# The gates of four chunks, two chunks at a time, by seven block products in place of eight

## Chip, core and metric

The kernel runs on one core of one Trainium2 chip. The metric is the device time of one execution in microseconds, the median of several runs. The core's engines work in parallel, each through its own instruction queue and in order: TensorE (PE, with its weight loads shown as PEld), VectorE (DVE), ScalarE (ACT), GpSimd (POOL) and SyncE (SP), which here issues nearly all DMAs. Matrix products land in PSUM, which has eight banks of 128 x 512 float32; DVE and ACT read them from there.

## The reference

Linear attention over 8 batches of 8 heads, 576 positions and 64 dimensions, then a feed-forward layer whose hidden value is the largest of three products. Cut to what matters:

```python
q_s = softmax(q, axis=-1)          # over the 64 dimensions
k_s = softmax(k, axis=2)           # over the 576 positions
kv = np.einsum('bhsd,bhse->bhde', k_s, v)
attn = np.einsum('bhsd,bhde->bhse', q_s, kv)
x = attn.transpose(0, 2, 1, 3).reshape(4608, 512)
h = np.maximum(np.maximum(x @ w1, x @ w2), x @ w3)     # each w: 512 x 768
out = h @ w_out                                        # 768 x 512
```

The weights come as float64 and the result goes out as float32.

## The kernel before

**Precision.** A product of two float32 matrices is made of three matmuls in a rounded format (F32R): each operand is split into a high part, which ACT copies, and a low part, which DVE subtracts; low x high, high x low and high x high are added up in one PSUM bank.

**Chunks.** The 4608 rows of x are worked on in nine chunks of 512. Chunks 0 to 7 are the first 512 positions of the eight batches; chunk 8 holds the 64 left over of each batch (the tile `left`). x lies turned: the 512 inner values in four blocks of 128 partitions (`g`, one for each pair of heads), the 512 rows along the free dimension.

**Gates** (`Chunk.gate`, L821 to 838). For each of six blocks of 128 hidden features (`j`) and each of three weights (`i`), 4 inner blocks x 3 = 12 matmuls of 128x128 on 128x512 add up in one of four banks (pool `pf`): 216 matmuls a chunk. **Hidden** (`Chunk.hidden`, L840): ACT copies the first product out of its bank, DVE takes the maximum with the other two, ACT makes the high part, DVE the low part. **Second products** (`Chunk.second`, L863): for each of four tiles of 128 rows 6 x 3 = 18 matmuls, a copy by ACT (L892) and a store by SP (L899, L904), the last tile in two halves (L880, L883): 72 matmuls a chunk.

**Attention.** Each batch has four pairs of heads. For batches 2 to 7 a pair takes loads of k, q and v (14 DMAs with the transfers of `q`), DVE and ACT work for the two softmaxes, a 32x32 transpose by DVE into `tb` (L654), eight small SP transfers `qT<-tb` (L667) that finish the turning of q, a split of q (L676, L679), the k v product on PE (L532) and the product that gives x (`Pair.x_steps`, L714 to 762), six matmuls at L741. From its bank x is split into `xbuf[b % 2]`, so batch b's x waits for the gates of chunk b - 2 (L721), and 64 rows go to `left`. Batches 0 and 1 go another way, by PE transposes. `left_queries` (L764) makes the left-over rows of these two.

**Weights.** 24 slices of w1, w2, w3 and w_out are loaded as float64, joined to float32 and split into `wh`, `wl` and `wo` in the first 110 us or so; `wh` and `wl` then stay in SBUF.

**Order.** The whole order is made when the program is built. Every piece of work is a generator that yields steps (`Step`: engine, estimated cost, what it waits for, which buffers it takes and frees). The planner (`Streams.run`, L149) holds a clock for each engine and always issues the next step that can begin, the one of lowest rank where several can. Ranks are set at the end (L992 to 1038): chunk c's gates have 1000 + 100 c and its second products 50 more, hidden steps come first of all, attention has the low ranks in the order of batches. Each engine then runs its instructions in just this order on the chip, and waits where a semaphore isn't there yet. The banks of `pf` are passed on in one fixed sequence, `in_pf` (L311).

Of the kernel before, what the change touches and what calls it, by code (L numbers as in the profile page):

```python
# [49 lines left out]
X_F32 = False  # L50

# [153 lines left out]
def linear_attention_then_maxout_ffn(  # L205
# [43 lines left out]

    const = ctx.enter_context(tc.tile_pool(name="const", bufs=1))  # L250
    att = ctx.enter_context(tc.tile_pool(name="att", bufs=2))
    hp = ctx.enter_context(tc.tile_pool(name="hp", bufs=NJ))
# [4 lines left out]
    start_stack, early_stack, conv2_stack = ExitStack(), ExitStack(), ExitStack()  # L257
    start = start_stack.enter_context(tc.tile_pool(name="start", bufs=2, side="right"))

    wh = [const.tile([P, NC, DF], F32R, name=f"wh{i}") for i in range(3)]  # L260
    wl = [const.tile([P, NC, DF], F32R, name=f"wl{i}") for i in range(3)]
    wo = []
    left = const.tile([P, 2, NC, B * LEFT], F32R, name="left")
    xbuf = [const.tile([P, 2, NC, CH], F32R, name="x0")]
# [6 lines left out]
    early = early_stack.enter_context(tc.tile_pool(name="early", bufs=1))  # L271
    k0 = early.tile([P, 5, H, D], F32, name="k0")
    q0 = early.tile([P, H, 4, D], F32, name="q0")
    v0 = early.tile([P, H, 5, D], F32, name="v0")
# [8 lines left out]
    count = early.tile([P, P], F32, name="count")  # L283
    turned_count = early.tile([P, P], F32, name="turned_count")
# [27 lines left out]
    for c in range(B + 1):  # L312
        in_pf += [(c, j, i) for j in range(NJ) for i in range(3)] + [(c, "y", t) for t in range(4)]
    st = Streams({"pf": 4, "pa": BANKS[0], "sm": BANKS[1], "keT": 1, "hp": NJ, "tmp": 3, "ke": 2, "kep": 1, "qe": 2, "qf": 1, "qt": 2, "tb": 1, "qT": 2, "qhl": 1}, {"pf": in_pf, "tb": list(range(TURNED * NP, B * NP))})
    late_pools, turn_pools = [], []
# [3 lines left out]
    class Slice:  # L319
# [18 lines left out]
        def load(self, pool, nst, nx):  # L338
            t = pool.tile([P, NC, 2 * P], U32, name="wst", bufs=nst)
# [3 lines left out]
            self.pool, self.nx = pool, nx  # L343

        def join(self, room):
            n, low, high = self.n, self.low, self.high
            e = yield Step("AV", (0.56, 0.39), [("wst", n)], take=[(room, n)], port="V")
            x = self.x = self.pool.tile([P, CH], F32, name="wx", bufs=self.nx)
# [32 lines left out]


    class Pair:
# [330 lines left out]
        def x_steps(self):  # L714
# [6 lines left out]
            after = [("bd", n), ("qhl", n), ("gates", b - 2) if b >= 2 else None, "late" if b == 1 else None]  # L721
# [20 lines left out]
            h, lo = (xbuf[b % 2][:, i, self.g, :] for i in range(2))  # L742
# [6 lines left out]
            rest = CH - half  # L749
            yield Step("A", act(half))  # L750
            nc.scalar.copy(out=h[:, :half], in_=xT[:, :half])
            yield Step("A", act(rest))
            nc.scalar.copy(out=h[:, half:], in_=xT2[:, :rest])
            yield Step("V", dve(half), free=[room])
            nc.vector.tensor_sub(out=lo[:, :half], in0=xT[:, :half], in1=h[:, :half].bitcast(F32))
            yield Step("V", dve(rest), gives=("x", b, self.g))
            nc.vector.tensor_sub(out=lo[:, half:], in0=xT2[:, :rest], in1=h[:, half:].bitcast(F32))
            h, lo = (left[:, i, self.g, b * LEFT : (b + 1) * LEFT] for i in range(2))
            yield Step("A", act(LEFT))
            nc.scalar.copy(out=h, in_=xT2[:, rest:half])  # L760
            yield Step("V", dve(LEFT), free=[small], gives=("xl", b, self.g))
            nc.vector.tensor_sub(out=lo, in0=xT2[:, rest:half], in1=h.bitcast(F32))

    def left_queries():  # L764
# [41 lines left out]
        h, lo = (left[:, i, :, 0 : TURNED * LEFT] for i in range(2))  # L806
        yield Step("A", act(CH))
        nc.scalar.copy(out=h, in_=xv)
        yield Step("V", dve(CH), free=room, gives="left")
        nc.vector.tensor_sub(out=lo, in0=xv, in1=h.bitcast(F32))  # L810


# [258 lines left out]
```

## Time and profile before

| | |
|---|---|
| median of three runs | 703.74 us (703.21 to 704.28) |
| the profiled execution | 704.3 us, span 702.2 us |
| matmul instructions | 3542 |
| DMA bytes moved | 58.06 MB, 83280 packets |
| HBM read, written | 40.89 MB, 9.44 MB |
| gate matmuls, mean duration | 392 ns (wh), 398 ns (wl) |

The span is the time from the first to the last instruction; 2.1 us of the execution lie around it. A matmul's duration is longer than the spacing of two, since matmuls overlap. In the page, the slices cut the span in forty parts, each digit a share in tenths. In the chain that ended last each row is a start, a length, the engine and the line, with the number of instructions merged. In a group's row the columns after the bar are the total busy time, the mean of one in ns, and the idle time before them with its releaser. In the windows each engine's busy time stands with its instruction count, then PE's granted clock, the share of the DMA engines and GB/s.

### The profile page before, as it was taken

Reading aid. Unit: us, or ns where it says so; the run is one execution under the profiler, and the core shown is the slowest. Engines: PE = TensorE matmul, PEld = TensorE weight load, DVE = VectorE, ACT = ScalarE, POOL = GpSimd, SP = SyncE. Lnnn points to the kernel's source line nnn. Section 1 sums busy time; section 2 is a strip of 40 time slices with the busy share of each in tenths; the row PEclk is TensorE's granted clock in tenths of the full one; section 3 lists DMA queues with packets and bytes.
Section 4 is the critical chain, followed back from the end, with each engine's and each line's share of the span. In section 5 each row is a group of like instructions: output and inputs, shape, how many; then the busy total and the mean of one; then the engine's idle time right before and its main releaser. Section 6 shows DMA issues by size and latency. Waiting matters only on the chain.

```text
span 702.2 us, 9785 instructions
## 1 busy us (share of the span) xinstructions
PE 675.4 (96%) x3542; PEld 551.7 (79%) x3542; DVE 398.5 (57%) x804; ACT 249.1 (35%) x578; POOL 58.5 (8%) x75
## 2 busy tenths in 40 slices
PE   3589999999999999999999999999999999999997
PEld 2467877888888888888888888888888888888885
DVE  6689988789869797795588258623222112201220
ACT  5579866334344334331442135113211111111111
POOL 3223222301100000010000000000000000000000
PEclk9789999999999999999999999999999999999999
DMA  8748433443462443440253024101100000010002
GB/s 238 201 147 243 148 95 106 145 107 97 130 167 69 113 116 102 127 112 15 74 153 105 1 70 126 34 1 33 45 1 1 30 31 0 1 46 15 1 0 61
DMA packets 83280, 58.06 MB, mean 83 GB/s; under 512 B 49184, under 2 KB 74784, under 8 KB 83232
## 3 DMA queue, kind: packets, MB, share of 16 engines
q1 hardware_dynamic: 83152, 57.31, 28.9%
q8 instruction: 28, 0.46, 0.3%
q14 instruction: 20, 0.16, 0.1%
q10 hardware_dynamic: 80, 0.13, 0.0%
HBM read 40.89 MB, written 9.44 MB: 72 GB/s over the span
## 4 chain that ended last, share of the span: by engine, by line
PE 93%; DMA 2%; SPq 1%; DVE 1%; ACT 1%; issue 0%; ACTq 0%; DVEq 0%
PE pf L835 64%; PE pf L874 21%; DMA wst<-in_moe_w_dram 2%; PE pa L532 2%; PE pa L741 2%; PE sm L741 1%; PE sm L575 0%; SPq L930 0%; PE pa L464 0%; PE pa L703 0%; PE pa L689 0%; SPq L418 0%; PE pa L804 0%; SPq L933 0%; DVE wl L379 0%
## 5 line engine op out<-in xcount | busy, mean ns | idle before, releaser
L835 PE MATMUL pf<-x,wh 128*128 128x512 f32 x1152 | 358.5, 392 | 0.0
L835 PEld LDWEIGHTS pf<-x,wh 128*128 128x128 f32 x1152 | 216.8, 188 | 47.6 <-issue 0.2
L835 PE MATMUL pf<-x,wl 128*128 128x512 f32 x576 | 229.1, 398 | 0.7 <-ACT bdf L587 0.7
L847 DVE TENSOR_TENSOR m<-pf,m 128x512 f32<-128x512 f32 x108 | 74.4, 689 | 188.0 <-PE pf L835 185.8
L835 PEld LDWEIGHTS pf<-x,wl 128*128 128x128 f32 x576 | 108.4, 188 | 24.9 <-ACT bdf L587 0.9
L850 ACT CAST h_h<-m 128x512 fp32r<-128x512 f32 x54 | 33.5, 620 | 182.4 <-DVE m L847 182.4
L874 PE MATMUL pf<-ol,h_h 128*128 128x512 f32 x216 | 86.2, 399 | 0.0
L874 PE MATMUL pf<-oh,h_l 128*128 128x512 f32 x216 | 84.4, 391 | 0.0
L874 PE MATMUL pf<-oh,h_h 128*128 128x512 f32 x216 | 84.4, 391 | 0.0
L844 ACT COPY m<-pf 128x512 f32<-128x512 f32 x54 | 31.6, 586 | 57.0 <-PE pf L835 52.5
L854 DVE TENSOR_TENSOR h_l<-m,h_h 128x512 fp32r<-128x512 f32 x54 | 37.1, 687 | 19.2 <-ACT h_h L850 19.2
L874 PEld LDWEIGHTS pf<-ol,h_h 128*128 128x128 f32 x216 | 40.6, 188 | 8.8 <-issue 0.7
L874 PEld LDWEIGHTS pf<-oh,h_l 128*128 128x128 f32 x216 | 40.5, 188 | 8.6
L874 PEld LDWEIGHTS pf<-oh,h_h 128*128 128x128 f32 x216 | 40.7, 188 | 8.4 <-issue 0.7
L835 PE MATMUL pf<-left,wh 128*128 128x512 f32 x144 | 44.3, 389 | 0.0
L502 POOL PARTITION_ALL_REDUCE kma<-km x24 | 19.0, 793 | 281.3 <-DVE km L499 131.0
L892 ACT COPY m<-pf 128x512 f32<-128x512 f32 x35 | 20.5, 587 | 56.8 <-PE pf L874 56.3
L364 POOL TENSOR_TENSOR wst<-wx,wst 128x512 int32<-128x512 int32 x24 | 31.3, 1305 | 87.7 <-DVE wx L360 52.8
L654 DVE STREAM_TRANSPOSE tb<-qt 128x576 f32<-128x576 f32 x24 | 30.7, 1281 | 5.4 <-DMA qT<-tb 5.2
L835 PEld LDWEIGHTS pf<-left,wh 128*128 128x128 f32 x144 | 27.0, 188 | 5.6
L835 PE MATMUL pf<-left,wl 128*128 128x512 f32 x72 | 28.0, 389 | 0.0
L679 DVE TENSOR_TENSOR q_l<-qT,q_h 128x576 fp32r<-128x576 f32 x24 | 18.1, 754 | 16.6 <-ACT q_h L676 15.9
(154 smaller groups left out, 671.7 us busy)
## 6 DMA issues: line engine op xcount, KB each, us to landing
wst<-in_moe_w_dram SPq DMA_DIRECT2D x18, 512.0 KB, 4.8
out_dram<-m SPq DMA_DIRECT2D x32, 256.0 KB, 2.2
vt<-in_v_dram SPq DMA_DIRECT2D x56, 128.0 KB, 3.0
qt<-in_q_dram SPq DMA_DIRECT2D x24, 288.0 KB, 3.2
qT<-tb SPq DMA_DIRECT2D x192, 36.0 KB, 1.9
kt<-in_k_dram SPq DMA_DIRECT2D x24, 256.0 KB, 3.1
wst<-in_moe_w_out_dram SPq DMA_DIRECT2D x6, 512.0 KB, 3.3
q<-in_q_dram SPq DMA_DIRECT2D x8, 256.0 KB, 5.5
```

The lines of the kernel that those rows point to most:

```text
L364: nc.gpsimd.tensor_add(out=low.bitcast(I32), in0=x.bitcast(I32), in1=low.bitcast(I32))
L502: nc.gpsimd.partition_all_reduce(kma, km, P, bass_isa.ReduceOp.max)
L654: nc.vector.transpose(out=tb.rearrange("p e (c s) -> p s e c", s=QS), in_=self.qt.rearrange("p s (e c) -> p s e c", e=2))
L679: nc.vector.tensor_sub(out=q_l, in0=self.qT, in1=q_h.bitcast(F32))
L741: nc.tensor.matmul(out=out, lhsT=l, rhs=r[:, cs], start=(i == 0), stop=(i == last))
L835: nc.tensor.matmul(out=ps, lhsT=l[:, cc, js], rhs=r, start=(cc == 0 and t == 0), stop=(cc == NC - 1 and t == 2))
L844: nc.scalar.copy(out=m, in_=self.m.pop((j, 0)))
L847: nc.vector.tensor_max(out=m, in0=self.m.pop((j, i)), in1=m)
L850: nc.scalar.copy(out=h, in_=m)
L854: unit[e].tensor_sub(out=lo, in0=m, in1=h.bitcast(F32))
L874: nc.tensor.matmul(out=po, lhsT=l, rhs=r[:, j, :], start=(j == 0 and i == 0), stop=(j == NJ - 1 and i == 2))
L892: nc.scalar.copy(out=o, in_=po)
```

## The change

Chunks 0 to 4 stay as they were. Chunks 5 and 6, and 7 and 8, are worked on as two pairs (`Duo`). A pair's gates are seen as 2 x 2 blocks: two feature blocks of 128 (j = 2jp and 2jp + 1) by two halves of the inner dimension for a weight, two halves of the inner dimension by two chunks for x. With weight blocks A, x blocks B, and S, T for their sums,

```
S1 = A21 + A22   S2 = S1 - A11   S3 = A11 - A21   S4 = A12 - S2
T1 = B12 - B11   T2 = B22 - T1   T3 = B22 - B12   T4 = B21 - T2
P1 = A11 B11  P2 = A12 B21  P3 = S4 B22  P4 = A22 T4  P5 = S1 T1  P6 = S2 T2  P7 = S3 T3
U = P1 + P6   C11 = P1 + P2   C12 = U + P5 + P3   C22 = U + P5 + P7   C21 = U + P7 + P4
```

Each product is six matmuls (2 inner blocks x 3 terms), where the four outputs took 48. There are nine block pairs `u` (three jp, three weights), so 63 products for each pair of chunks.

- *Weight blocks.* For each u the three plain blocks, high and low, are stored from `wh`, `wl` to DRAM (`prepare_weights`, six DMAs of 128 KB), and the four sums are formed by DVE (six operations and two for the low parts) and ACT (two) and stored (`mix_weights`, two DMAs). Each product then loads its block of 256 KB into one of ten buffers `ws`.
- *x.* Batches 5, 6 and 7 keep x unsplit (`xf`, ACT copies only), as does `left`. `Duo.convert` forms the four sums on DVE and splits seven blocks into `xb`, which lies where the weights were. x of batches 5 and 6 waits for the gates of chunk 3, of batch 7 for the first pair's conversion (`x_free`).
- *Banks.* Four banks: `a` holds P1 and then P1 + P2; `c` holds P5 and then P5 + P3; two others in turn are seeded by ACT with P1 and take P6, P7 and P4. Between products ACT and DVE read or copy them and take the maxima into `mm`.
- *Second products* run after all nine u of a pair, eight tiles, each split first into one of two buffers `hs`.
- *Places.* Most tiles move into one slab with offsets by hand, so that the new ones can share space with weights, x and hidden tiles that are done with.
- `left_queries` gets rank 230, where it had 301.

```diff
+PAIRED = 5
+LEFT_AT, PREP_AT, PREP_STEP = 230.0, 280.0, 0.5
...
+    W_AT, X0_AT, SCR_AT, H_AT, E_AT = 0, 73728, 90112, 98304, 122880
+    xbuf = [place(f"x{i}", [P, 2, NC, CH], F32R, at) for i, at in enumerate((X0_AT, E_AT))]
+    hp_h = Placed("h_h", [P, CH], F32R, H_AT, NJ)
+    wo = [place(nm, [P, NJ, DM], F32R, E_AT + 16384 + 12288 * i) for i, nm in enumerate(("oh", "ol"))]
+    xf = [place(f"xf{i}", [P, NC, CH], F32, E_AT + 8192 * i) for i in range(2)]
+    xb = [place(f"xb{i}", [P, 2, 2, CH], F32R, W_AT + 8192 * i) for i in range(7)]
+    ws = [place(f"ws{i}", [P, 2, 2, P], F32R, SCR_AT + 2048 * i if i < 4 else W_AT + 57344 + 2048 * (i - 4)) for i in (0, 1, *range(4, 12))]
+    mm = place("mm", [P, 2, NJ, CH], F32, H_AT)
+    hs = [place(f"hs{i}", [P, 2, NJ, P], F32R, X0_AT + 6144 * i) for i in range(2)]
+    wd = [dram.tile([P, 7, 2, 2, P], F32, name=f"wd{u}") for u in range(9)]
...
+    for u in range(10):
+        turn = [("P1", u), ("P5", u), ("P4", u - 1), ("P6", u), ("P2", u), ("P3", u), ("P7", u)]
+        wino_order += [(p, n) for p, n in turn if 0 <= n < 9]
...
+    def x_free(b):
+        if b < 2:
+            return None
+        if b < PAIRED:
+            return ("gates", b - 2)
+        return ("gates", PAIRED - 2) if b < PAIRED + 2 else ("conv", b - 2 - (b - PAIRED) % 2)
...
-            after = [("bd", n), ("qhl", n), ("gates", b - 2) if b >= 2 else None, "late" if b == 1 else None]
+            after = [("bd", n), ("qhl", n), x_free(b), "late" if b == 1 else None]
...
+            else:
+                yield Step("A", act(half), free=[room])
+                nc.scalar.copy(out=x[:, :half], in_=xT[:, :half])
+                yield Step("A", act(rest), gives=("x", b, self.g))
+                nc.scalar.copy(out=x[:, half:], in_=xT2[:, :rest])
...
+    WINO = {"P1": (0, 0), "P5": (6, 1), "P2": (1, 2), "P6": (3, 3), "P7": (5, 4), "P3": (4, 5), "P4": (2, 6)}
...
+    def mix_weights():
...
+            for r in range(2):
+                yield Step("V", dve(CH), ["turn", "left", ("split", 6 * jp + i), ("split", 6 * jp + 3 + i)], port="V")
+                nc.vector.tensor_tensor(out=v[:, r], in0=hv[:, r].bitcast(F32), in1=lv[:, r].bitcast(F32), op=ALU.add)
+            for o, x, y, op in (
+                (a22, a21, a22, ALU.add), (a21, a11, a21, ALU.subtract), (a11, a22, a11, ALU.subtract),
+                (a12, a12, a11, ALU.subtract),
+            ):
+                yield Step("V", dve(256), port="V")
+                nc.vector.tensor_tensor(out=o, in0=x, in1=y, op=op)
...
+            for hl, t in enumerate((mix_h, mix_l)):
+                yield Step("S", 0.64, kb=512, gives=("mixed", u) if hl else None)
...
+    class Duo:
...
+        def convert(self):
+            c = self.c
+            before = [("gates", PAIRED - 1), *(("kept", u) for u in range(9))] if c == PAIRED else [("gates", c - 2)]
...
+            def split(i, src, after, gives):
+                yield Step("A", act(2 * CH), [*before, *after])
+                nc.scalar.copy(out=xb[i][:, 0], in_=src)
+                yield Step("V", dve(2 * CH), gives=("cv", c, i), port="V")
+                nc.vector.tensor_tensor(out=xb[i][:, 1], in0=src, in1=xb[i][:, 0].bitcast(F32), op=ALU.subtract)
...
+        def weights(self, at):
+            c = self.c
+            for n, (p, u) in enumerate(self.order):
+                slot = (at + n) % len(ws)
+                first = c == PAIRED and n < len(ws)
+                after = [("mixed", u), ("kept", u), (("mixed", 8) if slot < 2 else ("gates", PAIRED - 1)) if first else None]
+                yield Step("S", 0.64, after, take=[("ws", (c, p, u))], gives=("w", c, p, u), kb=256)
+                nc.sync.dma_start(out=ws[slot].bitcast(F32), in_=wd[u][:, WINO[p][0]])
...
+        def products(self, at):
...
+                need = {
+                    "P1": ("c11", u - 1), "P5": ("c12", u - 1), "P2": ("sb", u), "P6": ("sb", u), "P7": ("u2", u),
+                    "P3": ("s5", u), "P4": ("c22", u),
+                }[p]
...
+                yield Step("T", 6 * f32r(CH), after, take=take, free=[("ws", (c, p, u))], gives=(p, c, u))
...
+                terms = [(k, a, b) for k in range(2) for a, b in ((1, 0), (0, 1), (0, 0))]
+                for i, (k, a, b) in enumerate(terms):
                     nc.tensor.matmul(
+                        out=bank[on], lhsT=w[:, a, k], rhs=x[:, b, k], start=(i == 0 and p in ("P1", "P5")), stop=(i == 5),
+                        skip_group_check=True,
                     )
...
+            return [
+                seeded(),
+                copied("c", s5[u % 2], [("P5", c, u), ago("d22")], ("s5", c, u)),
+                also(alone("a", m11, [("P2", c, u), *(old or ())], ("c11", c, u), bank_free(0, u == 8)), ("d11", c, u)),
+                copied(sb, u2[u % 2], [("P6", c, u), ago("d12")], ("u2", c, u)),
+                with_copy("c", u2[u % 2], m12, [("P3", c, u), ("u2", c, u)], ("c12", c, u), bank_free(1, u == 8), ("d12", c, u)),
+                with_copy(sb, s5[u % 2], m22, [("P7", c, u), ("s5", c, u)], ("c22", c, u), done=("d22", c, u)),
+                alone(sb, m21, [("P4", c, u)], ("c21", c, u), bank_free(2 + u % 2, u >= 7)),
+                met(),
+            ]
...
-    st.add(left_queries(), FIRST + CHUNK * 4)
+    st.add(left_queries(), LEFT_AT)
+    st.add(prepare_weights(), LEFT_AT)
+    st.add(mix_weights(), PREP_AT, PREP_STEP)
...
+    for n, d in enumerate(duos):
+        r = GATES_AT + 100.0 * (PAIRED + 2 * n)
+        for i, g in enumerate(d.convert()):
+            st.add(g, -900.0 + i)
...
+        st.add(d.weights(len(d.order) * n), r - 2000.0)
+        st.add(d.products(len(d.order) * n), r)
+        for u in range(9):
+            for g in d.outcome(u):
+                st.add(g, -1500.0 + u)
...
+        for t in range(8):
+            st.add(d.hidden(t), -1000.0 + t)
+            st.add(d.second(t), r + 50 + t)
```

More of the change, by code (lines that the diff above doesn't have):

```diff
@@ L805, in left_queries @@
         xv = xT.rearrange("p (g t) -> p g t", g=NP)
[L806 to L810, printed above, removed]
+        yield Step("A", act(CH), free=room, gives="left")
+        nc.scalar.copy(out=left[:, :, 0 : TURNED * LEFT], in_=xv)
     class Chunk:
@@ L863, in second @@
         def second(self, t):
-            c, ts = self.c, slice(t * P, (t + 1) * P)
-            for j in range(NJ):
-                key = ("pf", (c, "y", t))
-                yield Step(
-                    "T", 3 * f32r(CH), [("h", c, j), ("split", NG + j)], take=[key] if j == 0 else (), gives=("y", c, t, j)
-                )
-                if j == 0:
-                    po = pf.tile([P, CH], F32, name="pf")
-                hh, hl = self.hh[j][:, ts], self.hl[j][:, ts]
-                for i, (l, r) in enumerate(((hh, wo[1]), (hh, wo[0]), (hl, wo[0]))):
+            ts = slice(t * P, (t + 1) * P)
@@ new lines, in linear_attention_then_maxout_ffn, with prepare_weights @@
+    WINO = {"P1": (0, 0), "P5": (6, 1), "P2": (1, 2), "P6": (3, 3), "P7": (5, 4), "P3": (4, 5), "P4": (2, 6)}
+    def prepare_weights():
+        for u in range(9):
+            jp, i = divmod(u, 3)
+            js = slice(2 * jp * P, 2 * (jp + 1) * P)
+            hv, lv = (t[i][:, :, js].rearrange("p c (r n) -> p r c n", r=2) for t in (wh, wl))
+            yield Step("S", 0.64, ["turn", ("split", 6 * jp + i), ("split", 6 * jp + 3 + i)], kb=128)
+            for part, (block, r, cc) in enumerate(((0, 0, 0), (1, 0, 2), (2, 1, 2))):
+                for hl, t in enumerate((hv, lv)):
+                    if part or hl:
+                        yield Step("S", 0.64, kb=128, gives=("kept", u) if part == 2 and hl else None)
+                    nc.sync.dma_start(out=wd[u][:, block, hl], in_=t[:, r, cc : cc + 2].bitcast(F32))
@@ new lines, in all_gates, with hidden @@
+        def all_gates(self):
+            yield Step("-", 0.0, [("P4", self.c, 8), ("P3", self.c, 8)], gives=("gates", self.c))
+        def hidden(self, t):
+            c = self.c
+            h, q = self.tiles[t]
+            ts = slice(q * P, (q + 1) * P)
+            o = hs[t % 2]
+            for part, jj in enumerate((slice(0, 4), slice(4, NJ))):
+                n = (jj.stop - jj.start) * P
+                yield Step("A", act(n), [("m", c, 5), ("m", c, 8) if part else None], take=[("hs", (c, t))] if not part else ())
+                nc.scalar.copy(out=o[:, 0, jj], in_=mm[:, h, jj, ts])
+                yield Step("V", dve(n), gives=("hl", c, t, part), port="V")
+                nc.vector.tensor_tensor(
+                    out=o[:, 1, jj], in0=mm[:, h, jj, ts], in1=o[:, 0, jj].bitcast(F32), op=ALU.subtract
+                )
@@ L908, in linear_attention_then_maxout_ffn, with second @@
+        def second(self, t):
+            h, q = self.tiles[t]
+            o = hs[t % 2]
+            yield from second_product(
+                self.c, t, lambda j: (o[:, 0, j], o[:, 1, j]), lambda j: [("hl", self.c, t, 0 if j < 4 else 1)],
+                self.c + h, q, last=self.c + 2 > B and t == 7, done=("hs", (self.c, t)),
+            )
     pairs = {(b, g): Pair(b, g) for b in range(B) for g in range(NP)}
     slices = [Slice(n) for n in range(NS)]
-    chunks = [Chunk(c) for c in range(B + 1)]
+    chunks = [Chunk(c) for c in range(PAIRED)]
@@ L911, in linear_attention_then_maxout_ffn @@
+    duos = [Duo(c) for c in range(PAIRED, B + 1, 2)]
     N_ST, N_X, N_ST2, N_X2 = ROOMS
```

297 lines of the change are left out of this document (219 added, 78 removed).

## The prediction

> **What bounds the kernel now.** I read the totals and the forty slices first, then the chain that ended last in order of time, then the groups of instructions by shape.
>
> ```profile
> span 702.2 us, 9785 instructions
> PE 675.4 (96%) x3542; PEld 551.7 (79%) x3542; DVE 398.5 (57%) x804; ACT 249.1 (35%) x578; POOL 58.5 (8%) x75
> PEclk9789999999999999999999999999999999999999
> DMA  8748433443462443440253024101100000010002
> GB/s 238 201 147 243 148 95 106 145 107 97 130 167 69 113 116 102 127 112 15 74 153 105 1 70 126 34 1 33 45 1 1 30 31 0 1 46 15 1 0 61
> PE 93%; DMA 2%; SPq 1%; DVE 1%; ACT 1%; issue 0%; ACTq 0%; DVEq 0%
> ```
>
> PE is busy 96% of the span and carries 93% of the chain. From the third slice on nothing else decides. So the change is worth what it takes out of PE's stream, less every gap that it opens there. The chain from chunk 4's second products to the end:
>
> ```profile
> 406.45 1.36 PE pf L874 x6
> 429.00 50.38 PE pf L835 x216
> 500.60 49.01 PE pf L835 x216
> 549.61 16.33 PE pf L874 x72
> 565.94 50.20 PE pf L835 x216
> 616.14 16.33 PE pf L874 x72
> 632.47 48.97 PE pf L835 x216
> 681.44 16.34 PE pf L874 x72
> 697.85 0.44 DVE m L880
> ```
>
> There are no gaps: 216 gate matmuls a chunk, 72 second ones, the next chunk. 48.97/216 = 0.2267 us a matmul, and 16.33/72 = 0.2268. Chunks 5 and 7 take 0.2333 and 0.2324: they read x from the other of the two buffers. I can't say from this trace what in that buffer costs 2.5%, so it is carried as a pace of its own.
>
> **The change part by part.**
>
> *Removed.* The gates of chunks 5 to 8: 50.38 + 49.01 + 50.20 + 48.97 = 198.6 us, 864 matmuls.
>
> *Added on PE.* Seven products of six matmuls for each of nine block pairs, twice: 2 x 9 x 42 = 756 matmuls of the same shape. At 0.2267 they take 171.4 us, at 0.2333 176.4 us. Net -27.2 us at the better pace. The second products stay at 72 per chunk, and attention's matmuls stay too.
>
> *Pace.* x, the weight blocks, the hidden tiles and the output weights all get new places, so any stage may run at either pace. If chunks 1 and 3 lose the slow pace, that is 2 x (50.2 - 49.0) = -2.4 us. If the products and all nine chunks' second products (648 x 0.0066 = 4.3 us) get it, that is 5.0 + 4.3 = +9.3 us. I take **+2**, near the pace that most of the rows have.
>
> *Handovers inside a product turn.* Each bank is drained or seeded between two products that use it: P1 is copied by ACT into the third bank before P6 adds to it, P6 is read before P7, P7 before P4, P2 before the next P1, P3 before the next P5. Each time two other products, twelve matmuls, lie between: 2.72 us (P5 to P3 has three). PE works in the written order, so whatever stands behind a product that waits, waits too. What the reading takes:
>
> ```profile
> 672.65 0.61 PE L835 MATMUL pf<-left,wh 128*128 128x512 f32 x2
> 673.11 0.39 PE L835 MATMUL pf<-left,wl 128*128 128x512 f32 x1
> 673.31 0.69 DVE L847 TENSOR_TENSOR m<-pf,m 128x512 f32<-128x512 f32 x1 [1.96 <-PE pf L835]
> 674.03 0.62 ACT L850 CAST h_h<-m 128x512 fp32r<-128x512 f32 x1 [5.52 <-DVE m L847]
> L844 ACT COPY m<-pf 128x512 f32<-128x512 f32 x54 | 31.6, 586 | 57.0 <-PE pf L835 52.5 <-issue 4.1
> L654 DVE STREAM_TRANSPOSE tb<-qt 128x576 f32<-128x576 f32 x24 | 30.7, 1281 | 5.4 <-DMA qT<-tb 5.2
> ```
>
> DVE starts 0.20 us after the next group's first matmul (673.31 against 673.11), works 0.69, and the next engine starts 0.03 later. So a handover needs about 0.9 to 1.0 us out of 2.72. It has 1.7 us to spare, more than one 1.28 us transpose of batch 7 in front of it. DVE's load in a turn is six operations of 0.69 (two where i = 0): 3 x 1.4 + 6 x 4.1 = 29 us of 86. Price: 0 if they fit; if a transpose and another operation stand in front at one handover in each turn, 0.3 us x 18 = 5. I take **+1**.
>
> *Weight blocks from DRAM.* 63 loads of 256 KB for each pair, one per product (1.36 us): 193 GB/s.
>
> ```profile
> 600.00:650.00 50.00, 50.00 (x221) 41.11 (x220) 8.44 (x13) 7.63 (x13) 0.00 (x0) 1.00 0.06 22
> 406.40:429.00 22.60, 22.60 (x178) 18.94 (x176) 13.89 (x31) 11.13 (x28) 0.70 (x1) 1.00 0.39 106
> out_dram<-m SPq DMA_DIRECT2D x32, 256.0 KB, 2.2
> wst<-in_moe_w_out_dram SPq DMA_DIRECT2D x6, 512.0 KB, 3.3
> ```
>
> In the windows (last two columns: DMA share, GB/s) 2 KB rows go at 22/0.06 = 370 GB/s of a full DMA, and in the fourth slice 243 GB/s were really moved at a share of 0.8. So the loads take some 0.55 of the DMA, and with attention's densest stage (0.39) still under 1. Ten buffers let a load run 13.6 us ahead, against 2.2 to 3.3 us to land. Price 0, covered by that lead; bounds 0 and +5, should the two overlap for a whole pair.
>
> *Before the first pair: the crowd.* The block sums need eight DVE operations in each of nine rounds, 9 x (4 x 0.69 + 4 x 0.41) = 40 us of DVE, and 18 ACT copies. SP gets 54 + 18 DMAs to issue, at 0.63 each 34 + 11 us. Batch 6's x, which waited for chunk 4's gates, is now needed as those end, to be converted together with batch 5's.
>
> ```profile
> L497 DVE TENSOR_TENSOR kh<-kt 128x256 f32<-128x256 f32 x24 | 9.8, 409 | 2.2 <-DMA kt<-in_k_dram 2.2
> 200.00:250.00 50.00, 50.00 (x298) 41.60 (x298) 39.17 (x83) 18.80 (x41) 2.11 (x3) 1.00 0.41 107
> 250.00:300.00 50.00, 50.00 (x302) 41.51 (x301) 40.00 (x85) 20.76 (x44) 3.11 (x4) 1.00 0.45 121
> 300.00:334.70 34.70, 34.70 (x155) 28.14 (x155) 24.99 (x46) 8.83 (x14) 1.77 (x2) 1.00 0.20 53
> 334.70:357.20 22.50, 22.50 (x178) 18.86 (x176) 13.84 (x31) 11.07 (x27) 0.70 (x1) 1.00 0.37 106
> 357.20:406.40 49.20, 49.20 (x219) 40.74 (x218) 31.03 (x60) 11.86 (x21) 2.40 (x3) 1.00 0.26 70
> 227.76 5.01 SPq L667 DMA_DIRECT2D qT<-tb  x8
> 313.88 26.51 SPq L667 DMA_DIRECT2D qT<-tb  x11
> L741 PE MATMUL pa<-q_l,bdh x8: 292/296/300, 152.0 to 238.6; 128*128 128x288 f32 x8
> 362.48 5.24 SPq L667 DMA_DIRECT2D qT<-tb  x7
> 375.28 36.81 SPq L667 DMA_DIRECT2D qT<-tb  x11
> ```
>
> DVE (third busy figure) is idle 10.8 + 10.0 + 9.7 + 8.7 + 18.2 = 57 us between 200 and 406.4, so 40 us fit on paper, and some 0.8 us a pair goes away with the low parts of x for batches 5 and 6. Is the last pair in time? Pairs of heads follow each other by 12.8 us (375.28 - 362.48). The last of batch 6 began its qT transfers at 375.28, right behind the third, and was then held inside the 36.81 us row until chunk 4's gates had freed room. Not held, it starts near 388, and its x comes 10.8 us after (227.76 to 238.6): 399. Gates of chunk 4 end at 406.45, some 4 us later when batch 6's own matmuls have moved ahead of them, and the second products cover another 16.3. In those the convert needs DVE for ten operations of 1024 elements, which I estimate at 1.25 us each (0.41 for 256, 0.69 for 512), 12.5 us, and the first two products wait for three of them. So about 20 us of slack stand against 85 us of added work on two engines, most of which falls into their idle time. The transfers that were held within rows of 26.51 and 36.81 us show that SP had room, too. Price 0 if the idle time is used well; +15 if 35 of the 85 us find no idle time and come after the slack of 20. I take **+3**, near the end that the idle rows speak for.
>
> *At the end of each pair.* The hidden tiles need all nine rounds. P4 of the last round waits for P7's reading, 1.0 us, and the last two blocks of the first second products then need a max, a copy and a subtraction, 0.9 + 0.4 + 0.4 us. Ready beside it are the first four blocks of two tiles, 2 x 12 x 0.2268 = 5.4 us: covered. The third tile waits for one of two buffers, about 1.7 us after the first tile ends, with 1.4 us of the second left: 0.3 to 1 us. From both sides 0 to 3 for each pair; I take **+2** for both. In the last pair the same tail follows as before (from 697.85 on).
>
> *Sum.* 704.3 in the profiled execution (span 702.2 and 2.1 around it) - 27.2 + 2 + 1 + 0 + 3 + 2 = 685.1. The median of the three runs, 703.74, lies 0.56 below the profiled one: **684.5 us**.
>
> **The rivals.**
>
> *The better case.* The new places run at the fast pace and the covers hold: 703.7 - 27.2 - 2.4 to + 1: 674 to 677. For it speaks how gapless the chain is; against it, that three kinds of waits are new and each has only some 2 us to spare.
>
> *Gaps remain.* Late x for the first pair by 10 to 15 us, or a handover missed in every turn: 688 to 700.
>
> *The clock.* PE that waits a little at every handover could lose clock. What slower means here:
>
> ```profile
> L464 PE MATMUL pa<-ident,k 128*128 128x128 f32 x16 | 4.3, 422 | 5.8 <-DMA k<-in_k_dram 5.8
> L464 PE MATMUL pa<-ident,kt 128*128 128x128 f32 x16 | 2.4, 272 | 0.0
> ```
>
> The same transposes took 422 ns in the first slices, where PEclk shows 7 to 9, and 272 later: 1.55 times. A quarter of the products at that rate costs 0.25 x 0.55 x 171.4 = 24 us: 708. Against it: the gates pass four banks on all the time and PEclk stays at 9, because the next bank is always free. The Trainium skill, "TensorE: Matmul & The Clock Gate", A second HAM failure mode: psum-queue depth-cycling, speaks for this rival: it tells of a kernel that cycled through its banks, where PE idled between groups often enough for the clock to fall and rise again. So far the trace doesn't agree, as the gates cycle through banks without loss.
>
> *The loads bound.* A load that comes every 2.2 us, the time of one 256 KB transfer, gives 126 x 2.2 = 277 us of loads against 171 of products: 790. It turns the sign from 1.58 us a load on (1.36 + 27.2/126). The fourth slice, where 512 KB loads overlap at 243 GB/s (1.08 us for 256 KB), speaks against it. The Trainium skill, "DMA: Bandwidth & Descriptors", Rules for kernel authors, asks for 1 MiB per DMA for full bandwidth; these have a quarter of that.
>
> *Slower by the crowd.* One mechanism before the first pair can turn the sign: SP issues in order, a store of block sums waits there for DVE, and batch 6's q transfers wait behind it; PE's products wait for batch 6's x. Every microsecond by which the last x comes more than the 20 us of slack after 399 is a microsecond of idle PE. It decides from 27 us beyond the slack on, when nearly all of the 85 us find no idle time: 704 to 715. Against it stand 57 us of idle DVE and the two held transfers.
>
> *It doesn't do what it says.* If the planner put the products later than the code's ranks say, nothing would be saved and 703.7 stays; so would it if the gaps eat just what is saved.
>
> **How the numbers follow.** The forecast, 678 to 688: 0.50. The better case, 674 to 678: 0.17. Gaps, 688 to 700: 0.19. The clock: 0.04. The loads: 0.01. The crowd: 0.06. No change: 0.03. The range 675 to 698 leaves out the last four, 0.14, and the edges of the second and third. A measurement of this kernel can tell about 0.2%, 1.4 us. Faster by more than that: 0.50 + 0.17 + 0.19 = 0.86; within it 0.03; slower 0.04 + 0.01 + 0.06 = 0.11.
>
> **What would show it.** Two stretches of 378 product matmuls of about 86 us each in the chain, with 145 us of second products, attention and tail around them after chunk 4's gates; PE's waits for DVE or ACT in the products under 2 us in all; no PE wait on the block loads. If the first pair starts more than 20 us after chunk 4's last gate, the crowd was mis-sized. If PEclk shows anything but 9 past slice 3, the clock's case holds. If the products' mean spacing is 0.233, the pace term was.

## The result and the profile after

The changed kernel takes **677.38 us** (median of four runs, 676.41 to 678.42) against 704.01 for the kernel before on the same chip: a ratio of 0.9624 (95% interval 0.9605 to 0.9642), 26.6 us less. The forecast was 684.5 with a range of 675 to 698. The sign, the mechanism and the range held; the time itself lies in the rival called the better case.

The page of the changed kernel, profiled in its slowest run (678.42 us, span 676.6): totals, slices, the chain's shares, the group of the products and a row of the DMA issues. In this kernel L894 is the gate line, L1103 the products, L941 the second products, L799 the matmuls that give x.

```profile
span 676.6 us, 10151 instructions
PE 646.9 (96%) x3434; PEld 530.3 (78%) x3434; DVE 463.5 (68%) x893; ACT 293.3 (43%) x660; POOL 61.4 (9%) x75
PEclk9979999999999999999999999999999999999999
DMA  9757634365755434554575646876665126766021
PE 87%; SPq 5%; DMA 4%; DVE 2%; issue 1%; ACT 1%; DVEq 0%; ACTq 0%
...
L1103 PE MATMUL pf<-xb,ws 128*128 128x512 f32 x756 | 173.1, 389 | 0.0
...
ws<-wd SPq DMA_DIRECT2D x126, 256.0 KB, 3.0
```

PE is as full as before (96%), with 28.5 us less to do. DVE went from 398.5 to 463.5 us, and the DMA's slices show 5 to 8 while the products run, where that part of the span showed 0 to 2; PE waits for neither in the products, whose row has 0.0 us of idle time. PEclk stays at 9 after the third slice. PE's share of the chain fell from 93 to 87%: in two places before the products, near 200 and near 285, the chain now runs through SP and loads of q.

Where the time went is seen when both spans are cut at the end of chunk 4's second products, where the first pair begins. The windows of the kernel before and of the changed one, PE alone (length, then busy time with its instruction count):

```profile
0.00:429.00 429.00, 406.60 (x2327) 0.98 0.43 121
429.00:702.20 273.20, 268.76 (x1216) 1.00 0.08 23
```

```profile
0.00:428.70 428.70, 404.35 (x2326) 0.99 0.58 165
428.70:676.60 247.90, 242.51 (x1109) 1.00 0.52 149
```

Up to the cut the same number of matmuls was done in the same time, 0.3 us less, though block sums, stores and batch 6's x came on top. After it 273.2 us became 247.9: 25.3 of the 25.6 us by which the span is shorter lie behind the cut. PE's idle time there grew by 1.0 us, from 4.4 to 5.4.

The chain of the changed kernel from that place on (start, length, what):

```profile
428.90 14.96 PE pf L1103 x66
...
479.94 38.11 PE pf L1103 x168
518.05 2.04 PE pf L941 x9
520.09 1.37 PE pf L1103 x6
521.49 0.69 DVE mm L1132
...
527.42 1.02 issue
528.44 0.70 DVE hs L1187
529.18 24.34 PE pf L941 x106
553.53 84.32 PE pf L1103 x372
...
641.25 31.02 PE pf L941 x135
```

84.32/372 = 0.2267 us a product matmul: the better pace, with no gap in 62 products. Only the end of the first pair leaves PE: second products had begun (nine at 518), the last product P4 ended, and then DVE stands in the chain. PE's waits name the one pause:

```profile
PE pf L941 <- DVE hs L1187: 1.0, 1, 1.0
```

It is the third tile's buffer `hs`, as the prediction had it, but made longer by something it had not: the second pair's conversion, set free by `("gates", 5)`, puts operations of 1.2 us in front of `hs` on DVE. The timeline of DVE at that place:

```profile
526.17 1.22 DVE L1055 TENSOR_TENSOR xf<-left,bdf 128x1024 f32<-128x1024 f32 x1
527.30 1.23 DVE L1051 TENSOR_TENSOR xb<-left,xb 128x1024 fp32r<-128x1024 f32 x1
528.44 1.29 DVE L1187 TENSOR_TENSOR hs<-mm,hs 128x512 fp32r<-128x512 f32 x2
```

The crowd before the first pair fitted, but much more tightly than forecast. DVE (third busy figure) had 8.7 + 18.2 us of idle time in the two windows 334.7 to 406.4 before; now:

```profile
300.00:354.00 54.00, 54.00 (x316) 44.96 (x315) 52.20 (x110) 24.30 (x52) 4.12 (x4) 1.00 0.57 160
354.00:410.20 56.20, 56.20 (x328) 46.90 (x327) 52.23 (x103) 26.92 (x57) 2.11 (x3) 1.00 0.56 163
```

52 of 54 and of 56 us; in the same two windows the kernel before has 36.1 and 35.8. The last x of batch 6 is made at 421.6, where the working said 399, and its conversion ends just in time. The timeline of PE (L799 makes x), then that of DVE:

```profile
422.27 0.29 PE L799 MATMUL sm<-q_h,bdh 128*128 128x288 f32 x1
428.74 1.98 PE L1103 MATMUL pf<-xb,ws 128*128 128x512 f32 x8
```

```profile
424.29 1.22 DVE L1055 TENSOR_TENSOR xf<-xf 128x1024 f32<-128x1024 f32 x1
425.98 1.23 DVE L1051 TENSOR_TENSOR xb<-bdf,xb 128x1024 fp32r<-128x1024 f32 x1 [0.47 <-ACT xb L1049]
```

The second product (P5, about 430.2) needs the block that is ready at 427.2. About 3 us of the 20 us of slack are left.

The lateness begins long before the first block sum (228.3). From 175.6 to 196.7 SP issues 32 stores of plain blocks, about half a microsecond each, and neither a load of k nor a transfer of q among them. DVE runs dry behind them, as its timeline shows, and so do the windows from 186 to 205 (DVE alone, the kernel before and then the changed one):

```profile
204.56 0.42 DVE L555 TENSOR_TENSOR kh<-kt 128x256 f32<-128x256 f32 x1 [17.73 <-DMA kt<-in_k_dram]
```

```profile
186.00:205.00 19.00, 16.30 (x38) 1.00 0.65 181
186.00:205.00 19.00, 1.12 (x2) 1.00 0.61 184
```

The fourth of the 24 pairs of heads of batches 2 to 7 gets its x at 209.0, where it came at 190.0 before. PE had other work meanwhile: from 205 to 291 it idles 1.2 us, where before it idled 0.0.

### The profile page after: what moved, and what is told of

Read it like the earlier page. It is cut to its first block, busy times and chain, and to the rows that moved or that the text cites. A ratio compares the mean times of both kernels' runs of the same rounds, so it can differ in the third digit from the quotient of the medians.

```text
span 676.6 us, 10151 instructions
## 1 busy us (share of the span) xinstructions
PE 646.9 (96%) x3434; PEld 530.3 (78%) x3434; DVE 463.5 (68%) x893; ACT 293.3 (43%) x660; POOL 61.4 (9%) x75
## 4 chain that ended last, share of the span: by engine, by line
PE 87%; SPq 5%; DMA 4%; DVE 2%; issue 1%; ACT 1%; DVEq 0%; ACTq 0%
PE pf L894 34%; PE pf L1103 25%; PE pf L941 20%; DMA wst<-in_moe_w_dram 2%; PE pa L799 2%; PE pa L590 2%; PE sm L799 1%; DMA qt<-in_q_dram 1%; SPq L725 1%; DMA vt<-in_v_dram 1%; SPq L1224 1%; SPq L476 1%; PE sm L633 1%; DVE xb L1051 1%; SPq L1227 0%
## 5 line engine op out<-in xcount | busy, mean ns | idle before, releaser
L894 PE MATMUL pf<-x,wh 128*128 128x512 f32 x720 | 222.6, 390 | 0.0
L1103 PE MATMUL pf<-xb,ws 128*128 128x512 f32 x756 | 173.1, 389 | 0.0
L1103 PEld LDWEIGHTS pf<-xb,ws 128*128 128x128 f32 x756 | 141.6, 188 | 29.3
L894 PEld LDWEIGHTS pf<-x,wh 128*128 128x128 f32 x720 | 135.4, 188 | 27.5 <-issue 0.2
L894 PE MATMUL pf<-x,wl 128*128 128x512 f32 x360 | 143.8, 399 | 1.5 <-ACT m L903 0.9
L894 PEld LDWEIGHTS pf<-x,wl 128*128 128x128 f32 x360 | 67.7, 188 | 16.4 <-ACT m L903 1.3
L941 PE MATMUL pf<-oh,hs 128*128 128x512 f32 x192 | 59.7, 390 | 1.0 <-DVE hs L1187 1.0
L941 PE MATMUL pf<-ol,h_h 128*128 128x512 f32 x120 | 48.5, 404 | 0.0
L941 PE MATMUL pf<-oh,h_l 128*128 128x512 f32 x120 | 46.8, 390 | 0.0
L941 PE MATMUL pf<-oh,h_h 128*128 128x512 f32 x120 | 46.8, 390 | 0.0
L941 PEld LDWEIGHTS pf<-oh,hs 128*128 128x128 f32 x192 | 36.0, 188 | 9.3 <-DVE hs L1187 1.9
L941 PE MATMUL pf<-ol,hs 128*128 128x512 f32 x96 | 37.6, 392 | 0.0
L941 PEld LDWEIGHTS pf<-ol,h_h 128*128 128x128 f32 x120 | 22.5, 188 | 5.2 <-issue 0.7
```

Of the source, the lines that this page charges most:

```text
L894: nc.tensor.matmul(out=ps, lhsT=l[:, cc, js], rhs=r, start=(cc == 0 and t == 0), stop=(cc == NC - 1 and t == 2))
L941: nc.tensor.matmul(out=po, lhsT=l, rhs=r[:, j, :], start=(j == 0 and i == 0), stop=(j == NJ - 1 and i == 2))
L1103: nc.tensor.matmul(out=bank[on], lhsT=w[:, a, k], rhs=x[:, b, k], start=(i == 0 and p in ("P1", "P5")), stop=(i == 5), skip_group_check=True,)
```

## The experiments

The kernel before stands beside each on the same chip, at 703.6 to 704.5 us. The theory in all: PE's stream decides, and a cost counts only where its cover ends. The rivals differ by experiment.

**1. One pair.** Only chunks 7 and 8 are paired.

```diff
-PAIRED = 5
+PAIRED = 7
```

> Only chunks 7 and 8 are a pair; chunks 5 and 6 go chunk by chunk. Theory A, the time is PE's list of matmuls and all else is covered: half of the saving. Gates of chunks 7 and 8 took 50.20 + 48.97 = 99.2 us, 378 products at 0.2267 take 85.7, less 0.7 at the pair's end: 12.8 us faster than before, 691 us. Theory B, a pair's first cost (stores, block sums, conversion) is paid on the path once: the first pair alone gains less than half, 694 to 698 us.

689.00 us (688.01 to 690.17), ratio 0.979 (0.9774 to 0.9805). By chunk 7's and 8's rows of before, 99.2 us of gates become 85.7: 13.5 us less; 14.9 were gained. Chunk 5's gates, still 216 matmuls, lost most of their slow pace too (46.47 us for the last 204 of them, 0.2278 each), which had cost 1.4. So gain goes with products, pair by pair, and there is no fixed price of the whole arrangement.

**2. Block sums later.** The sums get later ranks, and so do the stores of the plain blocks and `left_queries`; the conversion and all first loads wait for the last sum.

```diff
-LEFT_AT, PREP_AT, PREP_STEP = 230.0, 280.0, 0.5
+LEFT_AT, PREP_AT, PREP_STEP = 260.0, 320.0, 0.5
...
-            before = [("gates", PAIRED - 1), *(("kept", u) for u in range(9))] if c == PAIRED else [("gates", c - 2)]
+            before = [("gates", PAIRED - 1), ("mixed", 8), *(("kept", u) for u in range(9))] if c == PAIRED else [("gates", c - 2)]
...
-                after = [("mixed", u), ("kept", u), (("mixed", 8) if slot < 2 else ("gates", PAIRED - 1)) if first else None]
+                after = [("mixed", u), ("kept", u), ("mixed", 8) if first else None, ("gates", PAIRED - 1) if first and slot >= 2 else None]
```

> left_queries and the stores of plain blocks get rank 260, the block sums 320 to 365 in place of 280 to 325, so they stand behind batch 5 and among batch 6; the conversion and the first loads wait for the last sum by name. Theory A, the crowd before the first pair fills nearly all of its cover (the last x of batch 6 came at 421.6, some 3 us before the first pair would have waited): the first product comes 10 to 25 us late, 687 to 702 us, with idle PE between chunk 4's second products and the first product and nowhere else. Theory B, DVE's idle time takes the sums wherever they stand: under 680 us.

695.43 us (694.90 to 696.37), ratio 0.9882 (0.9867 to 0.9897): 18 us more than the change. PE's waits show one pause, before the first product; the page's clock and two windows (PE alone, then the clock) show what came of it:

```profile
PE pf L1103 <- DMA ws<-wd: 14.7, 1, 14.7
```

```profile
PEclk9979999999999999999999999699999999999999
```

```profile
428.50:432.00 3.50, 0.00 (x0) 0.95 0.80 275
436.00:440.00 4.00, 0.00 (x0) 0.50 0.75 252
```

PE runs out of work at 428.5, and from about 432 on the granted clock is half; the 6 of the slice is a mean. The profiled span is 16.5 us longer than the change's: 14.7 of pause and 1.8 more of PE's busy time. The last sum is stored at 437.4 (408.8 in the change), and the loads that wait for it go out after. So the sums are free while the last of them is stored by about 423, an estimate from 437.4 - 14.7. The last x of batch 6, on the other hand, came earlier here, at 407.4, and the fourth pair's at 189.5, as in the kernel before.

**3. No sums.** `mix_weights` without its four DVE operations per round; all other steps stay, in the order that the planner then gives them. (Plain blocks then stand in the places of the sums.)

```diff
-            for o, x, y, op in (
-                (a22, a21, a22, ALU.add), (a21, a11, a21, ALU.subtract), (a11, a22, a11, ALU.subtract),
-                (a12, a12, a11, ALU.subtract),
-            ):
-                yield Step("V", dve(256), port="V")
-                nc.vector.tensor_tensor(out=o, in0=x, in1=y, op=op)
```

> Leaves out the four DVE sums in each round of the block sums (plain blocks are split and stored in their place): 9 x 4 x 0.41 = 15 us less on DVE before the first pair. Theory A, covered work costs nothing: 676 to 679 us, and the last x of batch 6 comes several us earlier than 421.6. Theory B, the sums cost PE something in 200 to 300, where PE now idles 1.2 us: 674.5 to 676.

679.45 us (678.21 to 679.76), ratio 0.9649 (0.9632 to 0.9665). DVE has 13.6 us less to do (449.9) and the kernel isn't faster, so the work that was taken out had been covered. The other half of the expectation failed: the last x of batch 6 came at 425.5, not several us before 421.6 but 4 after it, though the last sum's parts were stored by 365. The planner arranges the rest differently with the steps gone. PE's products now wait twice for `xb`, 1.4 us together, which is what 4 us do to a slack of 3.

**4. Three pairs.** Chunks 3 to 8 are paired, so that the sums must be done, and batch 4's x be there, 140 us earlier. Same waits as in experiment 2.

```diff
-PAIRED = 5
-LEFT_AT, PREP_AT, PREP_STEP = 230.0, 280.0, 0.5
+PAIRED = 3
+LEFT_AT, PREP_AT, PREP_STEP = 60.0, 220.0, 0.5
```

> Chunks 3 to 8 as three pairs (54 matmuls, 12.2 us, fewer); sums and stores get lower ranks (60 and 220), the conversion and the first loads wait for the last sum by name. Theory A: the sums, the stores and the attention of batches 3 and 4 must now all be done by the end of chunk 2's gates near 255 us; batch 4's last x came at 308 with the sums still to do, so the first pair starts 50 us and more late: 700 to 735 us, slower than with two pairs and perhaps than before. Theory B, the added work always finds idle time: 665 to 670 us.

One run, 723.87 us: slower than before, though 54 matmuls more, some 12 us, are gone. PE's waits, the slices, and a window of PE alone:

```profile
PE pa L799 <- DVE q_l L737: 33.2, 6, 14.6
```

```profile
PE   3599999999979999126899999999999999999997
PEclk9979999999998999655999999999999999999999
```

```profile
213.50:220.50 7.00, 5.06 (x11) 0.51 0.33 93
```

PE waits for the halves of q that DVE has not come to: three of these pauses, 14.6, 7.4 and 8.0 us, lie between 291 and 327, and the three slices there show a clock of 5 to 6. The clock also halved earlier, from 213.5 to 220.5, around three short pauses of 1.9, 0.6 and 2.2 us between 208.9 and 215.2. This is what the rival "slower by the crowd" foretold (late x, idle PE, the sign turned), produced by one pair more; whether SP's order, as the rival has it, or DVE's own load made q late, this run doesn't separate.

**5. Handovers back to back.** P6 follows P1, whose sum seeds its bank, with nothing in between (bank numbers of `a` and `c` exchanged to suit).

```diff
-        turn = [("P1", u), ("P5", u), ("P4", u - 1), ("P6", u), ("P2", u), ("P3", u), ("P7", u)]
+        turn = [("P5", u), ("P4", u - 1), ("P1", u), ("P6", u), ("P2", u), ("P3", u), ("P7", u)]
```

> The turn is P5, P4, P1, P6, P2, P3, P7: nothing lies between P1 and P6, which needs ACT's copy of P1. Theory A, a handover takes 0.9 to 1.0 us after the last matmul of the giver (0.2 to ACT's start, 0.57 the copy, 0.1 to PE): 18 x 0.9 = 16 to 18 us more, 693 to 696 us, and PE waits for ACT at each P6. Theory B, the pauses cost clock too: PEclk falls below 9 in the products and the time is over 700 us. Theory C, PE hides it by running ahead: under 680 us.

694.93 us (693.94 to 696.73), ratio 0.9877 (0.9860 to 0.9894). PE's waits name the seed by ACT, 17 of the 18 turns:

```profile
PE pf L1103 <- ACT pf L1151: 11.7, 17, 0.7
```

17.6 us over 18 handovers are 0.98 us each, the 0.9 to 1.0 that the prediction read from 673.31 to 674.03. The listed 0.7 is less, since a matmul's recorded duration (0.39) reaches beyond the spacing (0.227); by the start times P6 begins 0.8 to 0.9 us late each time. PEclk stays at 9 in every slice after the third: pauses of 0.7 us, one every 10.5 us, don't lower the clock here. The Trainium skill, "TensorE: Matmul & The Clock Gate", A second HAM failure mode: psum-queue depth-cycling, tells of a clock that falls and rises where PE idles often between groups; this is the nearest test of that among these runs, and the trace doesn't show it.

**6. One product between.** (Bank numbers changed to suit.)

```diff
-        turn = [("P1", u), ("P5", u), ("P4", u - 1), ("P6", u), ("P2", u), ("P3", u), ("P7", u)]
+        turn = [("P1", u), ("P4", u - 1), ("P6", u), ("P5", u), ("P7", u), ("P2", u), ("P3", u)]
```

> The turn is P1, P4, P6, P5, P7, P2, P3: one product, 1.36 us, between P1 and P6, P6 and P7, P2 and the next P1 in place of two. Theory A, a handover needs 0.9 to 1.0 us: still covered, 677 to 680 us. Theory B, the two products were needed: 0.3 us or more at each of three handovers in 18 turns, over 690 us.

679.30 us (678.57 to 680.47), ratio 0.9653 (0.9639 to 0.9668), with three waits for the seed:

```profile
PE pf L1103 <- ACT pf L1151: 2.5, 3, 1.1
```

Two of the three are the first turns of the pairs, where there is no P4 of a round before and P6 follows P1 directly: nothing lies between. In the third, at 473.9, a cast of attention's q stood before the seed on ACT, after ACT had waited 3.4 us for its transfer. All other turns have no such wait, so one product of 1.36 us covers a handover of 1.0. The 1.9 us by which the median lies above the change's are of the size of these waits, and the intervals of the two ratios overlap.

**7 and 8. Four and three block buffers** in place of ten.

```diff
-... for i in (0, 1, *range(4, 12))]
+... for i in (0, 1, 4, 5)]
```

> Four buffers for the weight blocks in place of ten. Theory A, a load takes 3.0 us from issue to landing and 0.1 us to be issued, so a buffer's round is 1.36 + 3.1 = 4.5 us against four products, 5.4 us: covered, 677 to 681 us. Theory B, loads that meet attention's DMAs in the first pair need more lead: first pair 5 us or more longer, second not, 682 to 690 us.

> Three buffers in place of ten. Theory A: a buffer's round of 4.5 us against three products, 4.08 us: 0.13 us more for each of 126 products, 17 us, 692 to 698 us, and PE waits for the block loads. Theory B, the issue queue's order adds to it: over 705 us. Theory C, a load's landing is mostly semaphore time that overlaps: under 682 us.

Four: 682.39 us (680.52 to 682.98), ratio 0.9691 (0.9675 to 0.9707), 5.0 us lost. By the start times of the product matmuls 3.6 us of it lie in the first pair and 0.7 in the second: theory B's place, with less than its 5 us there. Three (`(0, 1, 4)`): 704.38 us (702.76 to 705.58), ratio 1.0003 (0.9992 to 1.0014): the whole gain is lost, more than theory A's 17 us and just under theory B's 705. PE's waits for three buffers, and a stretch of its chain:

```profile
PE pf L1103 <- DMA ws<-wd: 9.3, 11, 1.8
```

```profile
502.12 26.97 PE pf L1103 x108
```

The waits listed are only a third of the loss. The rest is spacing inside the stretches, 26.97/108 = 0.2497 us a matmul, and it is the same wait in smaller pieces: by the start times 23.5 of the 25.8 us by which the profiled span is longer come before the first or the second matmul of a product. 27.0 us over 126 products are 0.21 each, so a buffer comes round in 3 x (1.36 + 0.21) = 4.7 us: used for 1.36, landing in 2.7 (this run's median), and what is left, 0.6, between the release and the issue. Theory A had 0.1 there; the issue alone takes SP 0.32 us (the median of this line in the trace). Ten buffers give 13.6 us for a round of 4.7. In the changed kernel it is SP that waits for free buffers, 106 times.

**9. Places exchanged in the kernel before.** `x1` (x of the odd chunks) moves to where `left` lay, and `left` to where `x1` lay; nothing else changes.

```diff
-    left = const.tile([P, 2, NC, B * LEFT], F32R, name="left")
-    xbuf = [const.tile([P, 2, NC, CH], F32R, name="x0")]
+    xbuf = [const.tile([P, 2, NC, CH], F32R, name=nm) for nm in ("x1", "x0")][::-1]
+    lefts = []
...
-        xbuf.append(late.tile([P, 2, NC, CH], F32R, name="x1"))
+        lefts.append(late.tile([P, 2, NC, B * LEFT], F32R, name="left"))
```

> The kernel before, with the places of the odd chunks' x buffer and of the left-over rows' tile exchanged; nothing else. In the kernel before, chunks 1, 3, 5 and 7 ran at 0.2324 to 0.2333 us a gate matmul and chunks 4, 6 and 8 at 0.227. Theory A, the pace goes with the buffer's place: the odd chunks run at 0.227, chunk 8 at 0.232; 4 x 1.2 - 1.2 = 3.6 us faster, 700.4 us. Theory B, it goes with something else that alternates (the banks' turn, the state PE is in): 704.0 us, odd chunks still slow.

700.38 us (700.00 to 701.58), ratio 0.9958 (0.9943 to 0.9972). The chain's rows for chunks 5, 7 and 8:

```profile
425.86 49.20 PE pf L835 x216
...
561.63 48.97 PE pf L835 x216
626.93 50.20 PE pf L835 x216
```

50.38 and 50.20 became 49.20 and 48.97, and chunk 8, which had 48.97, took over the 50.20. The slow pace belongs to the place of the buffer.

**10. Hidden parts first.** The second pair's conversion waits for the third `hs` of the pair before it, not for the last product.

```diff
-... if c == PAIRED else [("gates", c - 2)]
+... if c == PAIRED else [("hl", c - 2, 2, 1)]
```

> The second pair's conversion waits until the third tile's hidden part is split, so that no 1.2 us operation of the conversion stands before it on DVE. Theory A: the one wait of the first pair's end, 1.0 us for DVE, falls to 0.3: 676.7 us. Theory B, the wait is the buffer's own chain: 677.4 us, unchanged.

676.31 us (675.20 to 677.24), ratio 0.9611 (0.9595 to 0.9627). The wait for `hs` is gone, and the chain has all second products of the first pair in one piece:

```profile
521.26 31.05 PE pf L941 x135
```

1.1 us less than the change's median, in the expected direction and of the expected size, but the intervals of the two ratios overlap; the removed wait is shown, the gain isn't. It is the lowest median of all.

**11. Places alone.** A kernel of its own: 64 rounds of 36 matmuls of this shape, weights and moving operand in each of eight places.

> Computes nothing of the reference: 64 rounds of 36 matmuls 128x128 on 128x512, weights at each of eight places in SBUF (28672 bytes per partition apart), the moving operand at each of the same eight. Theory A, the slow pace (0.232 us) belongs to pairs of a low and a high place with some border between them: a block pattern in the 8 x 8 table, same-side pairs at 0.2267. Theory B, it goes with the moving operand's place alone: whole columns slow. Theory C, with the start address within a smaller period: no block pattern, single cells slow or none.

The chain has one row for all of it: 522.24/2304 = 0.2267 us, and no pair of places differs.

```profile
24.67 522.24 PE pf L46 x2304
```

All eight places lay multiples of 2048 bytes apart. So what is left of "place" is the address within a smaller period. The addresses of the built kernel before (read from the program; a trace holds none) say the same: within 512 bytes, `wh`, `wl`, `x0` and `left` all start at 384, `x1` at 256.

**12. Shifts.** The operand x moved by 32 bytes at a time, near and far, then the weights by 128. (The far round at 384 has exactly the old distance of `x1` from the weights, 158592 bytes; the 448 bytes in the text below are a slip.)

> A kernel of its own, in place of the whole computation: 36 rounds of 36 matmuls in the gates' order of terms (low weights by x, high weights by the low part of x, high by high). In 16 rounds x starts 0, 32, ..., 480 bytes off the weights' phase within 512 bytes, 90112 bytes behind the weights; in 16 more the same 158208 bytes behind, where a shift of 384 bytes is nearly the place that the buffer of chunks 5 and 7 had (same phase, 448 bytes off); in four more the weights themselves are shifted by 128 bytes and x by 0, 128, 256, 384. Theory A, the pace goes with the difference of the two start phases within 512 bytes: 0.2267 us a matmul at no shift, and again where both are shifted by 128; about 0.2324 at a shift of 384, near and far alike. Theory B, it needs the far place and the phase: only the far rounds have slow ones. Theory C, neither: all 36 rounds at 0.2267, and what slowed chunks 5 and 7 is something that this kernel doesn't have.

The chain has one row for each round. L52 to L97 are the shifts 0, 32, ..., 480 near, three lines each; L100 to L145 the same far; L148 to L157 the weights shifted by 128 and x by 0, 128, 256, 384.

```profile
21.80 8.16 PE pf L52 x36
29.96 8.40 PE pf L55 x36
38.37 8.25 PE pf L58 x36
...
88.65 8.19 PE pf L76 x36
...
121.90 8.40 PE pf L88 x36
...
155.53 8.19 PE pf L100 x36
...
255.65 8.40 PE pf L136 x36
...
289.27 8.40 PE pf L148 x36
297.67 8.17 PE pf L151 x36
```

At no shift 8.16/36 = 0.2267, at 32 bytes (L55) 0.2333, at 64 (L58) 0.2292, at 256 (L76) 0.2275, at 384 (L88) 0.2333. Far is like near (L100, L136). With both shifted by 128 (L151) it is fast again, and with the weights alone (L148) slow. Theory A holds, with a period of 256 bytes and not 512: x shifted by 256 is as good as x not shifted, within 0.4%.

## Why the prediction was right, and where it was high

The mechanism was right: PE's stream decides, 864 matmuls became 756, and nothing opened a gap of its size. The four allowances of the sum held 8 us; the profiled execution took 678.4, 25.9 less than before, so all that stands against the 27.2 is 1.3 us. Point by point:

- **Removed and added, -27.2: right.** The second stretch has 84.32/372 = 0.2267. In the windows PE's busy time behind the cut fell by 26.25; the 1 us between the two is in rows that I can't set apart.
- **Pace, +2: measured -2.25, the term that was off most.** It was carried as a chance of place. It can be read from addresses: in the changed kernel all operands of the gates and products lie in one slab at multiples of 2048 bytes, so none has a differing phase, and both stretches run at the good pace. Experiments 9 and 12 show the cause, 11 alone would have hidden it. It even gave something back: PE's busy time before the cut fell by 2.25 us with the same count of matmuls (406.60 to 404.35), as chunks 1 and 3 lost the slow pace (-2.4 in the bounds). But 2 us more of idle time before the cut took it: 0.75 in the first 60 us, where nothing was added, and the crowd's 1.2.
- **Handovers, +1: measured 0.** No product waits for ACT or DVE. The price read from the rows (0.9 to 1.0 us) is what an uncovered one costs (experiment 5), and one product between is enough wherever there is one (6).
- **Block loads, 0: right.** No wait for `ws` at ten buffers. The lead of 13.6 us was the right cover to name. The landing of 3.0 us lies within the 2.2 to 3.3 used, but the bound of +5 is not where the danger ends: at three buffers the loss is 27 (8). The rival's price of one load every 2.2 us didn't come, since loads overlap: 126 went through at one per 1.36 us. So what the Trainium skill asks for in "DMA: Bandwidth & Descriptors", Rules for kernel authors, 1 MiB per DMA, wasn't needed here.
- **Crowd, +3: measured 1.2, and the way there was wrong.** PE's idle time from 205 to 291 is all that it cost, and that idle DVE would take the work was right. But the last x came at 421.6 and not at 399, 22 us late, and the slack of 20 was spent but for about 3. The step took SP to have room, from two transfers that were only held. SP's queue is where it begins: 32 stores in a row kept k's loads and q's transfers back, DVE stood idle for 17.73 us, and the fourth pair was 19 us late before a single sum was made. Where the stores rank lower it wasn't late (189.5, experiment 2). The sums' time on DVE alone doesn't explain the rest: without 13.6 us of it the last x came no earlier (425.5, experiment 3). How the 22 us divide between SP's stores, the sums and the planner's order, no run shows. That some slack was left was luck: 4 us more of lateness cost 1.4 us (3), late sums cost 18 (2), and one pair more made the kernel slower than before (4). The mechanism of the rival "slower by the crowd", SP's order, was at work, and the cover was long enough.
- **Pair ends, +2: measured 1.0**, in the first pair alone, at the place named (the third tile's buffer). The second pair's conversion on DVE, which the step had not counted, stands in it: with that moved behind, the wait is gone (10).
- **The clock's rival: fell here.** Regular short pauses of 0.7 us leave PEclk at 9 (5). It isn't safe for good: a pause of 14.7 us halved the clock (2), and it was halved around three of 1.9, 0.6 and 2.2 us, too (4).
- **A sign that was wrong.** The 145 us set beside the products after chunk 4's gates don't follow from the rows: 702.2 - 406.45 - 198.6 leaves 97, and 95 were measured (676.6 - 410.2 - 171.4). The forecast doesn't use the figure.

Of the chances: 0.50 was given to 678 to 688 and 0.17 to the better case, 674 to 678, which came. Each allowance was a fear with a priced row and no chance of its own: one came the other way, one not at all, two at half their size or less, and all four were added up in full.

## What to carry to other kernels

Where one engine carries over 90% of the chain, count the instructions that leave its stream, and price each new wait by whether its cover is longer than it, not by a small sum for each. But work out how much of the cover remains: here 85 us of added work cost about 1 us and one pair more made the kernel slower than at the start. Look at each queue that others share, too: issues of half a microsecond, 32 in a row, held up loads that had nothing to do with them. When the same matmul has two durations in one kernel, compare the operands' start addresses modulo 256 bytes before blaming its neighbours.

## What the hardware showed that was not expected

- A 128x512 matmul's spacing depends on how the start addresses of its weights and its moving operand stand to each other within 256 bytes: 0.2267 us at the same phase, 0.2292 at 64 bytes, 0.2333 at 32, 128 and most others, 2.9% more (experiment 12). What in the chip does this no run shows.
- A pause of 14.7 us brought the granted clock to 0.50, from some 3 us after PE stopped (experiment 2). It was 0.51 from 213.5 to 220.5 around pauses of 1.9, 0.6 and 2.2 us, too (experiment 4, a single run), while 17 pauses of 0.7 us, one every 10.5 us, left it at 9 (5). Where between these the border lies, no run shows.
- Less work wasn't sooner: without 13.6 us of covered DVE work, in another order of steps, the last x came 4 us later and the median lay 2 us higher, with intervals that overlap (experiment 3). That the order is the cause was not tried.
